# Local attention and a gated MLP in one kernel: nine zero products ahead, a padded output chunk, transposes issued two tiles ahead, and the softmax division on GpSimd with its transpose issued later

## The chip, the cores and the metric

The kernel runs on 1 core of one Trainium2 chip. The metric is the device time of one execution in microseconds (us), the median of 3 runs.

A core has five engines that run side by side and wait for one another through semaphores: PE (TensorE: matrix products; the trace shows its weight loads apart, as PEld), DVE (VectorE), ACT (ScalarE), POOL (GpSimd) and SP (SyncE, which here only issues DMAs). Each engine takes its instructions in the order in which the program lists them.

## The reference: what is computed

One input x of 2048 tokens by 512, all in bf16. Both branches read the same normalised x, and both are added to x:

```python
xn = _layernorm(x, axis=-1)
return x + _A_ref(xn, A_wqkv, A_wo) + _B_ref(xn, B_w_in, B_w_sp, B_b_sp, B_w_out)
```

- A is attention with 32 heads of 16 dimensions. A token sees itself and the 255 tokens before it. Output: `softmax(q k^T / 4) v @ wo`.
- B is a gated MLP: `z = gelu(xn @ w_in)`, 1376 columns, split into z1 and z2 of 688; z2 is normalised per token; `g = w_sp @ z2 + b_sp` mixes all 2048 tokens; output: `(z1 * g) @ w_out`.

## The kernel before

Tokens are cut into 16 tiles of 128. Pools hold the on-chip tiles; PSUM, which PE writes, is divided into three pools: `ps_s` (3 buffers, tag S: scores), `ps_y` (one buffer, tag y: projections m, attention sums o_t, outputs fo) and `ps_g` (one buffer, tag g: mixing sums gf). With one buffer, the next user of y or g has to wait until an engine has copied the last one out.

**Stage 1** (to about 61 us of the span). For each token tile n: DVE takes mean and variance of x (`x_stats`, L387 and L388), POOL raises the variance to the power -0.5 (`rs_x`, L260), DVE normalises (`norm_apply`, L392). The result is transposed to xnT, for n below 8 by four PE products with the identity and a copy by ACT (`transpose_x`, L406 and L409), from 8 on by a DMA (L401). Then 16 products per tile and 1376 columns (`do_z`, L417) with gelu on ACT (L425); DVE takes the statistics of z2 (`z2_side`, L265) and normalises it (L269). The order is written out by hand (L443 to L516): x's statistics and norm run four and three tiles ahead, PE transposes one tile ahead, and from n = 6 on one early projection of k, q or v goes between the tiles. POOL also clears a few tiles there (`small_setup`, L377 to L381).

**Stage 2** (to about 283 us) works off a list of small groups, in an order that the class `Plan` (L41) computes before the program is built, from durations written into it (`OUT_MM`, the `td` added after an attention group, `o_at` from which an output group may be placed):

- `quad(kb, G, e)`: 4 score products of 32 rows each for a key block against up to 3 query blocks, into two S tiles; ACT takes exp into E (L631).
- `mask(kb, G)`: POOL clears the upper triangle of the diagonal block (L640), DVE multiplies the far block by a mask (L645).
- `unit_av(qb, half)`: 48 small products of E and v, the softmax sums among them, into o_t (L658). DVE then runs a series of four: transposes o_t to C (L667, tile o_c), takes the reciprocal of the sums (L671, rsum), multiplies (L673, o_norm) and transposes back (L680, oT).
- `unit_k`, `unit_q`, `unit_v`: projections of 4 products of 512 columns, copied out by DVE (L290, L310, L324).
- `unit_g(n, half, c)`: one of 16 products of the mixing with w_sp (L545); after the 16th, DVE forms u = (g + b) * z1 (L552), and after the second half a DMA transposes u to uT (L559).
- `unit_out(n, part)`: part 0 is 4 products of oT with wo (L585), part 1 is 6 products of uT with w_out (L593), of which the sixth has 48 rows; DVE adds x (L597), a DMA stores.

There are 512 g, 128 quad, 64 mask, 32 av, 37 projection and 26 output groups in the list. g groups are what the plan puts in where another group would have to wait.

**Tail**: output tiles 13, 14 and 15, one after another, in S tiles.

The series that the change takes apart:

```python
        nc.vector.reciprocal(out=rsum[:], in_=c_s)
        o_n = onp.tile([P, 8, 2, DH], BF, name="o_norm")
        nc.vector.tensor_tensor(out=o_n[:], in0=..., in1=..., op=ALU.mult)
        oT = otp.tile([P, 2, P], BF, name="oT")
        nc.vector.transpose(out=..., in_=...)
```

The functions that the diff touches, with their line numbers:

Of the kernel before, what the change touches and what calls it, by code (L numbers as in the profile page):

```python
# [8 lines left out]
P = 128  # L9
BF = mybir.dt.bfloat16  # L10
F32 = mybir.dt.float32
# [8 lines left out]
FH = 688  # L20
# [11 lines left out]
EBUFS = 12  # L32
X_DMA = 8
TAIL_OUT = 3


def nblk(kb):
# [3 lines left out]
class Plan:  # L41
# [1 line left out]

    PROJ = 0.91
    AV_PAIR = 0.0165
    OUT_MM = 0.24
    GCH = 0.144
    LAT = 0.36
    BACK = 0.08
# [13 lines left out]
    def run(self, proj, n_out_inline):  # L63
# [17 lines left out]
        while qi < len(quads) or ai < len(avs) or oi < len(outs) or gi < len(gs) or proj:  # L81
# [74 lines left out]
            if pick[2] == "quad":  # L156
                kb, G, e = quads[qi]
                w = nblk(kb)
                order.append(("quad", kb, G, e))
                a, b = (2 * qi) % 3, (2 * qi + 1) % 3  # L160
                dur = {3: 0.755, 2: 0.55, 1: 0.34}[w]
                lat = self.LAT - 0.05 * (3 - w)
                for s in (a, b):
                    self.ta = max(self.ta, self.tp + lat) + dur
                    self.sfree[s] = self.ta + self.BACK
                self.tp += 0.14 + 0.054 * w
                if e == 1:
                    pend.append((self.ta + 0.05, (kb, G)))
                qi += 1
            elif pick[2] == "av":  # L170
                qb, h = avs[ai]
                order.append(("av", qb, h))
                self.tp += pick[3]
                self.yfree = self.evac(0.75)
                self.td += 0.85
                if h == 1:
                    o_at[qb] = self.td + 0.1
                av_emitted.add((qb, h))
                ai += 1
            elif pick[2] == "proj":  # L180
                p = pick[4]
                proj.remove(p)
                order.append(("proj", p[2], p[3]))
                self.tp += pick[3]
                self.yfree = self.evac({"k": 1.2, "q": 0.7, "v": 0.7}[p[2]])
                done_proj[(p[2],) + p[3]] = self.yfree
            elif pick[2] == "out":
                n, part = outs[oi]
                order.append(("out", n, part))
                self.tp += pick[3]  # L190
                if part == 1:
                    self.yfree = self.evac(0.7)
                oi += 1
            else:
                n, hf, c = gs[gi]
                order.append(("g", n, hf, c))
                self.tp += self.GCH
                if c == NB - 1:
                    self.gfree = self.evac(0.52)
                    if hf == 1:  # L200
                        u_at[n] = self.gfree + 3.0
                gi += 1
# [6 lines left out]
def kernel(  # L209
# [102 lines left out]
    def unit_v(n, on_act=False):  # L312
# [10 lines left out]
        else:  # L323
            nc.vector.tensor_copy(out=dst, in_=src)  # L324

    nc.vector.memset(fmask[:], 1.0)
    nc.vector.memset(esel[:], 1.0)
    make_identity(nc, ident[:])
    with tc.tile_pool(name="win_pool", bufs=1) as winp, tc.tile_pool(
# [19 lines left out]
        def load_win(half, c0=0, c1=NDC):  # L349
# [23 lines left out]
            out=esel[:], in_=esel[:], pattern=[[32, 4]], compare_op=ALU.is_ge,  # L373
            fill=0.0, base=DH - 1, channel_multiplier=-1,
        )
        def small_setup():
            nc.gpsimd.memset(v_ring[:, :, :, 1, :], 1.0)  # L377
            for u_sb in u_sbs:
                nc.gpsimd.memset(u_sb[:, FH:UPAD], 0.0)
            with nc.allow_non_contiguous_dma(reason="tiny bias gather"):  # L380
                nc.gpsimd.dma_start(out=b_bf[:], in_=B_b_sp.rearrange("(n p) -> p n", p=P))  # L381

        xn_tiles = {}

# [13 lines left out]
        def transpose_x(n):  # L398
            xn = xn_tiles.pop(n)
            if n >= X_DMA:  # L400
                nc.sync.dma_start_transpose(out=xnT[:, :, n * P : (n + 1) * P], in_=xn[:])  # L401
                return
            pool, tag = (ps_y, "y") if n in (1, 3) else (ps_g, "g")
            tp = pool.tile([P, NDC, P], BF, name="tp", tag=tag)
            for c in range(NDC):
                nc.tensor.transpose(  # L406
                    out=tp[:, c, :], in_=xn[:, c * P : (c + 1) * P], identity=ident[:]
                )
            nc.scalar.copy(out=xnT[:, :, n * P : (n + 1) * P], in_=tp[:])  # L409

        def do_z(n, half):
            zp2 = ps_s.tile([P, 2, 512], F32, name="zs", tag="S")
            zp = zp2[:].rearrange("p a q -> p (a q)")
            f0 = half * FH
            for c in range(NDC):
                for lo, hi in Z_RANGES:
                    nc.tensor.matmul(  # L417
                        zp[:, lo:hi],
                        lhsT=xnT[:, c, n * P : (n + 1) * P],
                        rhs=w_in_sb[:, c, f0 + lo : f0 + hi],  # L420
                        start=(c == 0),
                        stop=(c == NDC - 1),
                    )
            dst = z1_all if half == 0 else z2_all
            nc.scalar.activation(out=dst[:, n, :], in_=zp[:, 0:FH], func=ACT.Gelu_apprx_tanh)  # L425
# [40 lines left out]
        nc.sync.dma_start(  # L466
            out=w_out_sb[:, 0:5, :], in_=B_w_out[0:640, :].rearrange("(c p) n -> p c n", p=P)
        )
        nc.sync.dma_start(out=w_out_sb[0:48, 5, :], in_=B_w_out[640:688, :])
        norm_apply(2)  # L470
        rs_x(3, 4)
        do_z(0, 1)
        norm_apply(3)
        do_z(1, 1)
        small_setup()
        transpose_x(2)
        x_stats(4)
        transpose_x(3)
        rs_x(4, 5)
        nc.vector.tensor_reduce(  # L480
            out=emask[:, 0:1], in_=esel[:], op=ALU.add, axis=mybir.AxisListType.X
# [9 lines left out]
        for n in range(2, NB + 3):  # L491
            if n < NB:
                do_z(n, 1)
            if n + 3 < NB:
                norm_apply(n + 3)
                if n + 3 >= X_DMA:
                    transpose_x(n + 3)
            if 3 <= n < X_DMA - 1:
                transpose_x(n + 1)
            if n == 4:  # L500
                nc.vector.tensor_copy(out=b_all[:], in_=b_bf[:])
            if 1 <= n - 1 < NB:
                z2_side(n - 1)
            if n + 4 < NB:
                x_stats(n + 4)
                rs_x(n + 4, n + 5)
            if n >= 6 and early:
                f, a = early.pop(0)
                f(*a, on_act=True)
            if n >= 3:  # L510
                do_z(n - 3, 0)
# [60 lines left out]
    def unit_out(n, part, tail=False):  # L572
        if part == 0:
            if not tail:
                load_xres(n)
            if tail:
                t = ps_s.tile([P, 2, 512], F32, name="mt", tag="S")
                fo_tiles[n] = t[:, 0, :]
            else:
                t = ps_y.tile([P, 512], F32, name="fo", tag="y")  # L580
                fo_tiles[n] = t[:]
            fo = fo_tiles[n]
            for c in range(NDC):
                oT = oT_tiles[(n, c // 2)]
                nc.tensor.matmul(  # L585
                    fo, lhsT=oT[:, c % 2, :], rhs=wo_sb[:, c, :], start=(c == 0), stop=False
                )
            return
        fo = fo_tiles.pop(n)
        uT = uT_tiles.pop(n)  # L590
        for c in range(NFC):
            kk = P if c < NFC - 1 else FH - (NFC - 1) * P
            nc.tensor.matmul(  # L593
                fo, lhsT=uT[0:kk, c, :], rhs=w_out_sb[0:kk, c, :], start=False, stop=(c == NFC - 1)
            )
        x_ch = x_tiles.pop(n)
        nc.vector.tensor_tensor(out=x_ch, in0=fo, in1=x_ch, op=ALU.add)  # L597
        (nc.scalar if tail else nc.sync).dma_start(out=out2[n * P : (n + 1) * P, :], in_=x_ch)
        if n + 1 < NB - TAIL_OUT:
            load_xres(n + 1)  # L600

    E_tiles = {}

    def quad(kb, G, e):
        nb = nblk(kb)
# [30 lines left out]
            )  # L636

    def mask(kb, G):
        E = E_tiles[(kb, G)]
        nc.gpsimd.affine_select(  # L640
            out=E[:, 0, :, :], in_=E[:, 0, :, :], pattern=[[0, 8], [1, P]], compare_op=ALU.is_ge,
            fill=0.0, base=0, channel_multiplier=-1,
        )
        if nblk(kb) == 3:
            nc.vector.tensor_tensor(  # L645
                out=E[:, 2, :, :], in0=E[:, 2, :, :],
                in1=fmask[:].unsqueeze(1).to_broadcast([P, 8, P]), op=ALU.mult,
            )

    def unit_av(qb, half):  # L650
        T = ps_y.tile([P, 2, 2 * P], F32, name="o_t", tag="y")
        kbs = [kb for kb in (qb - 2, qb - 1, qb) if kb >= 0]
        for g2 in range(2):
# [16 lines left out]
        rsum = sml.tile([P, 2, 8], F32, name="rsum")  # L670
        nc.vector.reciprocal(out=rsum[:], in_=c_s)  # L671
        o_n = onp.tile([P, 8, 2, DH], BF, name="o_norm")
        nc.vector.tensor_tensor(  # L673
            out=o_n[:],
            in0=c_o.rearrange("p e q d -> p q e d"),
            in1=rsum[:].rearrange("p e q -> p q e").unsqueeze(3).to_broadcast([P, 8, 2, DH]),
            op=ALU.mult,
        )
        oT = otp.tile([P, 2, P], BF, name="oT")
        nc.vector.transpose(  # L680
            out=oT[:].rearrange("p g q -> p (g q)"), in_=o_n[:].rearrange("p q e d -> p (q e d)")
        )
        oT_tiles[(qb, half)] = oT

    load_wsp(0)
    load_wsp(1)
# [65 lines left out]
```

## Time and profile before

| | |
|---|---|
| median of 3 runs | 295.42 us (295.39 to 295.44) |
| the profiled execution's own time | 295.57 us |
| its span, first to last instruction | 293.9 us |
| PE busy, share of the span | 269.4 us, 92% |
| ACT busy | 218.2 us, 74% |
| DVE busy | 213.9 us, 73% |
| POOL busy | 92.8 us, 32% |
| DVE row o_norm (L673), 32 of them | 21.4 us, 668 ns mean |
| POOL row mask (L640), 64 of them | 74.7 us, 1167 ns mean |
| DVE row mask (L645), 56 of them | 47.6 us, 853 ns mean |

Lnnn is a line of the kernel before. A row such as `L673 DVE TENSOR_TENSOR o_norm<-o_c,rsum` is one kind of instruction: its line, engine, operation, what it writes and what it reads. "Idle before" is the time for which the engine did nothing just ahead of it; "<-" names what ended that. [...]

### The profile page before, as it was taken

To read this page: it belongs to the slowest core of one execution; us is meant where nothing else is said; L and a number is where in the kernel's file an instruction comes from. 1 tells how busy PE (TensorE), PEld (TensorE's weight loads), DVE (VectorE), ACT (ScalarE), POOL (GpSimd) and SP (SyncE) were. 2 spreads that over 40 slices of the span, in tenths; PEclk is the share of its full clock that TensorE was granted. 3 is DMA by queue.
4 is the path that set the end of the run, shared out by engine and by line. 5 is a ranking of instruction groups with operands and counts; after the bars stand their busy time and mean duration, and the time that the engine had idled before them with its cause. 6 is when DMAs were issued, how large, how long until landed. Compare 5 with 4: busy or idle time off the path is not lost.

```text
span 293.9 us, 7526 instructions
## 1 busy us (share of the span) xinstructions
PE 269.4 (92%) x3136; PEld 135.5 (46%) x3168; DVE 213.9 (73%) x412; ACT 218.2 (74%) x314; POOL 92.8 (32%) x102
## 2 busy tenths in 40 slices
PE   1899999999989989999998999999898999999895
PEld 0555544444435444444544453545444554545451
DVE  5877777936877685865788887866869885956681
ACT  2478756588889889988699958783797678798810
POOL 3622222203342234324143323333233312335520
PEclk9999999999999999999999999999999999999999
DMA  7991111800415242332231423144314133545103
GB/s 230 324 284 44 36 38 36 170 12 0 100 19 118 65 72 51 89 85 51 65 74 39 99 44 94 39 97 56 83 36 100 31 70 83 94 38 134 29 4 80
DMA packets 60178, 23.58 MB, mean 80 GB/s; under 512 B 51264, under 2 KB 59632, under 8 KB 60144
## 3 DMA queue, kind: packets, MB, share of 16 engines
q1 hardware_dynamic: 59664, 22.70, 34.0%
q8 instruction: 25, 0.41, 0.6%
q10 hardware_dynamic: 432, 0.39, 0.4%
q0 software_dynamic: 48, 0.00, 0.1%
q14 instruction: 9, 0.07, 0.1%
HBM read 8.41 MB, written 2.10 MB: 36 GB/s over the span
## 4 chain that ended last, share of the span: by engine, by line
PE 64%; DVE 25%; issue 4%; POOL 3%; DMA 2%; ACT 1%; SPq 0%; DVEq 0%
PE gf L545 23%; PE S L623 9%; PE o_t L658 7%; PE fo L593 7%; PE fo L585 4%; PE m L315 4%; DVE st L265 3%; PE m L300 3%; DVE o_norm L673 3%; DVE st L387 3%; DVE o_c L667 3%; PE m L277 3%; DVE E L645 3%; POOL rstdx L260 2%; PE zs L417 2%
## 5 line engine op out<-in xcount | busy, mean ns | idle before, releaser
L631 ACT ACTIVATE E<-S 128x768 bf16<-128x768 f32 (+2 forms) x256 | 178.9, 773 | 38.4 <-issue 22.6
L640 POOL TENSOR_SCALAR_AFFINE_SELECT E<-E 128x1024 bf16<-128x1024 bf16 x64 | 74.7, 1167 | 147.9 <-ACT E L631 122.3
L545 PE MATMUL gf<-z_all,wspT 128*128 128x344 bf16 x512 | 94.6, 311 | 6.1 <-DVE u_sb L552 6.1
L545 PEld LDWEIGHTS <-wspT 128*128 128x128 bf16 x512 | 44.3, 97 | 38.4 <-issue 15.8
L645 DVE TENSOR_TENSOR E<-E,fmask 128x1024 bf16<-128x1024 bf16 x56 | 47.6, 853 | 0.6
L623 PE MATMUL S<-q_ring,k_ring 32*128 32x384 bf16 (+2 forms) x576 | 45.2, 303 | 1.3 <-ACT E L631 1.2
L417 PE MATMUL zs<-w_in_sb,xnT 128*128 128x512 bf16 (+1 forms) x251 | 42.5, 318 | 2.5 <-DMA xnT<-xn 1.3
L425 ACT ACTIVATE z_all<-zs 128x688 bf16<-128x688 f32 x32 | 23.8, 744 | 17.1 <-PE zs L417 17.1
L667 DVE STREAM_TRANSPOSE o_c<-o_t 128x512 f32<-128x512 f32 x32 | 22.9, 715 | 15.2 <-PE o_t L658 14.9
L417 PEld LDWEIGHTS <-xnT 128*128 128x128 bf16 x256 | 22.7, 101 | 20.9 <-DMA xnT<-xn 3.1
L623 PEld LDWEIGHTS <-k_ring 32*128 32x128 bf16 x576 | 14.6, 91 | 38.3 <-issue 36.0
L658 PE MATMUL o_t<-E,v_ring 128*32 128x128 bf16 x1440 | 26.0, 220 | 1.0 <-DVE k_ring L290 0.8
L658 PEld LDWEIGHTS <-v_ring 128*32 128x32 bf16 x1440 | 20.9, 97 | 8.2 <-issue 7.7
L597 DVE TENSOR_TENSOR x_ch<-fo,x_ch 128x512 bf16<-128x512 f32 x13 | 9.0, 692 | 21.2 <-PE fo L593 18.6
L673 DVE TENSOR_TENSOR o_norm<-o_c,rsum 128x256 bf16<-128x256 f32 x32 | 21.4, 668 | 1.1
L593 PE MATMUL fo<-w_out_sb,uT 128*128 128x512 bf16 x78 | 20.4, 382 | 0.0
L552 DVE SCALAR_TENSOR_TENSOR u_sb<-gf,b_all,z_all 128x344 bf16<-128x344 f32 x32 | 17.9, 560 | 1.7 <-PE gf L545 1.5
L290 DVE TENSOR_TENSOR k_ring<-m,emask 128x1024 bf16<-128x1024 f32 x12 | 14.7, 1221 | 5.8 <-PE m L277 5.8
L315 PE MATMUL m<-wqkv,xnT 128*128 128x512 bf16 x53 | 15.9, 381 | 1.1 <-DVE x_ch L597 0.5
L300 PE MATMUL m<-xnT,wqkv 128*128 128x512 bf16 x58 | 16.2, 380 | 0.7 <-DVE v_ring L324 0.3
L277 PE MATMUL m<-xnT,wqkv 128*128 128x512 bf16 x57 | 16.1, 380 | 0.6 <-DVE o_c L667 0.2
L260 POOL TENSOR_TENSOR rstdx<-rs_v,negh 128x1 f32<-128x1 f32 x16 | 8.8, 550 | 23.6 <-DVE rs_v L259 22.2
(51 smaller groups left out, 175.9 us busy)
## 6 DMA issues: line engine op xcount, KB each, us to landing
xs<-in_A_x_dram SPq DMA_DIRECT2D x7, 256.0 KB, 11.3
x_ch<-in_A_x_dram SPq DMA_DIRECT2D x13, 128.0 KB, 2.2
out_dram<-x_ch SPq DMA_DIRECT2D x13, 128.0 KB, 1.7
wqkv<-in_A_wqkv_dram SPq DMA_DIRECT2D x1, 1536.0 KB, 10.9
w_in_sb<-in_B_w_in_dram SPq DMA_DIRECT2D x4, 344.0 KB, 3.9
w_out_sb<-in_B_w_out_dram SPq DMA_DIRECT2D x1, 640.0 KB, 9.8
wo_sb<-in_A_wo_dram SPq DMA_DIRECT2D x1, 512.0 KB, 11.2
xnT<-in_A_x_dram SPq DMA_DIRECT2D x3, 128.0 KB, 3.3
```

Source lines behind the costliest of these rows:

```text
L300: nc.tensor.matmul(m[:], lhsT=wqkv[:, c, G * P : (G + 1) * P], rhs=xnT[:, c, grp * 512 : (grp + 1) * 512], start=(c == 0), stop=(c == NDC ...
L315: nc.tensor.matmul(m[:], lhsT=xnT[:, c, n * P : (n + 1) * P], rhs=wqkv[:, c, 2 * D : 3 * D], start=(c == 0), stop=(c == NDC - 1),)
L417: nc.tensor.matmul(zp[:, lo:hi], lhsT=xnT[:, c, n * P : (n + 1) * P], rhs=w_in_sb[:, c, f0 + lo : f0 + hi], start=(c == 0), stop=(c == NDC ...
L545: nc.tensor.matmul(gf[:, 0:FQ], lhsT=w[:, c, :], rhs=z2_all[:, c, lo : lo + FQ], start=(c == 0), stop=(c == NB - 1),)
L593: nc.tensor.matmul(fo, lhsT=uT[0:kk, c, :], rhs=w_out_sb[0:kk, c, :], start=False, stop=(c == NFC - 1))
L623: nc.tensor.matmul(S[:, i, d0 : d0 + w], lhsT=k_ring[32 * s : 32 * s + 32, G, e, k0 : k0 + P], rhs=q_ring[32 * s : 32 * s + 32, G, s0 : s0 ...
L631: nc.scalar.activation(out=E[:, 0:nb, j : j + 3 : 2, :].rearrange("p b h c -> p h b c"), in_=tiles[pr][:, :, 0:ncol].rearrange("p h (b c) ...
L640: nc.gpsimd.affine_select(out=E[:, 0, :, :], in_=E[:, 0, :, :], pattern=[[0, 8], [1, P]], compare_op=ALU.is_ge, fill=0.0, base=0, channel_ ...
L645: nc.vector.tensor_tensor(out=E[:, 2, :, :], in0=E[:, 2, :, :], in1=fmask[:].unsqueeze(1).to_broadcast([P, 8, P]), op=ALU.mult,)
L658: nc.tensor.matmul(T[32 * s : 32 * s + 32, e, g2 * P : (g2 + 1) * P], lhsT=v_ring[:, kb % VRING, 4 * G + s, e : e + 2, :].rearrange("p a d ...
L667: nc.vector.transpose(out=C[:, 0 : 32 * DH], in_=T[:].rearrange("p e q -> p (e q)"))
L673: nc.vector.tensor_tensor(out=o_n[:], in0=c_o.rearrange("p e q d -> p q e d"), in1=rsum[:].rearrange("p e q -> p q e").unsqueeze(3).to_bro ...
```

## The change

Four edits, the first three of which are independent of the fourth.

1. Nine products of 128x512 zeros are put at the head of PE's list, into an S tile that nothing reads. Their source is a slice of xnT that DVE clears first.
2. Chunk 5 of w_out, 48 rows, is cleared by POOL to 128 rows, so that the sixth product of an output's part 1 has 128 rows. uT's rows behind the 48 come from columns of u that were zero already. `OUT_MM` in the plan goes from 0.24 to 0.222.
3. `transpose_x` by PE runs two tiles ahead, and tiles 2 and 3 are transposed between the first two `do_z`. Tile 3 uses the g buffer.
4. The product with the reciprocals goes from DVE to POOL. The transpose behind it (oT) is not issued at once: `unit_av` puts it on a list `o_late`, and `finish_o` issues it at the next `unit_av`, at the output group that needs it, or at every second mask, whichever is first. In the plan, DVE's time after an av falls from 0.85 to 0.72 and `o_at` moves 2 us later, which makes another order of the whole list.

```diff
+    nc.vector.memset(xnT[:, 3, 0:512], 0.0)
...
+        nc.gpsimd.memset(w_out_sb[:, NFC - 1, :], 0.0)
...
+        wt = ps_s.tile([P, 2, 512], F32, name="warm_t", tag="S")
+        for i in range(N_WARM):
+            nc.tensor.matmul(
+                wt[:, 0, :], lhsT=xnT[:, 3, 0:P], rhs=xnT[:, 3, 0:512], start=True, stop=True
+            )
...
-            pool, tag = (ps_y, "y") if n in (1, 3) else (ps_g, "g")
+            pool, tag = (ps_y, "y") if n == 1 else (ps_g, "g")
...
         do_z(0, 1)
+        transpose_x(2)
         norm_apply(3)
         do_z(1, 1)
+        transpose_x(3)
         small_setup()
-        transpose_x(2)
         x_stats(4)
-        transpose_x(3)
...
-            if 3 <= n < X_DMA - 1:
-                transpose_x(n + 1)
+            if n + 2 < X_DMA:
+                transpose_x(n + 2)
...
-            kk = P if c < NFC - 1 else FH - (NFC - 1) * P
             nc.tensor.matmul(
-                fo, lhsT=uT[0:kk, c, :], rhs=w_out_sb[0:kk, c, :], start=False, stop=(c == NFC - 1)
+                fo, lhsT=uT[:, c, :], rhs=w_out_sb[:, c, :], start=False, stop=(c == NFC - 1)
             )
...
-    OUT_MM = 0.24
+    OUT_MM = 0.222
...
-                self.td += 0.85
+                self.td += 0.72
                 if h == 1:
-                    o_at[qb] = self.td + 0.1
+                    o_at[qb] = self.td + 2.0
...
             fo = fo_tiles[n]
+            if any(r[0] == n for r in o_late):
+                finish_o()
...
     def mask(kb, G):
+        if o_late and kb >= 0:
+            o_age[0] += 1
+            if o_age[0] % 2 == 0:
+                finish_o()
...
     def unit_av(qb, half):
+        finish_o()
...
-        nc.vector.tensor_tensor(
+        nc.gpsimd.tensor_tensor(
             out=o_n[:],
             in0=c_o.rearrange("p e q d -> p q e d"),
             in1=rsum[:].rearrange("p e q -> p q e").unsqueeze(3).to_broadcast([P, 8, 2, DH]),
             op=ALU.mult,
         )
-        oT = otp.tile([P, 2, P], BF, name="oT")
-        nc.vector.transpose(
-            out=oT[:].rearrange("p g q -> p (g q)"), in_=o_n[:].rearrange("p q e d -> p (q e d)")
-        )
-        oT_tiles[(qb, half)] = oT
+        o_late.append((qb, half, o_n))
+
+    def finish_o():
+        while o_late:
+            qb, half, o_n = o_late.pop(0)
+            oT = otp.tile([P, 2, P], BF, name="oT")
+            nc.vector.transpose(
+                out=oT[:].rearrange("p g q -> p (g q)"), in_=o_n[:].rearrange("p q e d -> p (q e d)")
+            )
+            oT_tiles[(qb, half)] = oT
```

More of the change, by code (lines that the diff above doesn't have):

```diff
@@ L34 @@
 TAIL_OUT = 3
+N_WARM = 9
 def nblk(kb):
@@ L468 @@
         )
-        nc.sync.dma_start(out=w_out_sb[0:48, 5, :], in_=B_w_out[640:688, :])
+        nc.sync.dma_start(out=w_out_sb[0 : FH - 5 * P, 5, :], in_=B_w_out[5 * P : FH, :])
         norm_apply(2)
@@ L602 @@
     E_tiles = {}
+    o_age = [0]
     def quad(kb, G, e):
@@ L648, in mask @@
             )
+    o_late = []
     def unit_av(qb, half):
+        finish_o()
         T = ps_y.tile([P, 2, 2 * P], F32, name="o_t", tag="y")
```

## The prediction, made before the changed kernel had run

> **What bounds the kernel.** I read the page's busy times first, then the chain of waits of the whole span, then the chain in two windows, then PE's own rows. PE is busy 92% of the span, and the chain by line is led by PE rows. But the chain changes hands between two stages, so each edit has to be priced in its own stage.
>
> Stage 1, the chain in the window 42 to 62 us (start, length, what):
>
> ```profile
> 50.57 0.41 DVE xn L392
> ...
> 51.02 2.42 DMA xnT<-xn
> ...
> 53.48 1.34 PE zs L417 x8
> ...
> 57.77 3.45 PE zs L417 x23
> 61.22 0.27 PE S L623 x4
> ```
>
> The same chain asked from 8 us on shows no PE row before 53.48: from 8.98 (POOL clearing v_ring, 0.90, then the issue of a DMA, 1.27) it goes round DVE and POOL only, 3.6 us per token tile (x's statistics start at 23.37, 27.23 and 30.60), while PE's own round, seen in four early projections at 26.88, 30.07, 33.27 and 36.47, takes 3.2. PE arrives early and waits for the last transposes by DMA. After the last one it has 7.7 us of fixed work, and stage 2 starts at 61.15.
>
> Stage 2, the chain in the window 207 to 213:
>
> ```profile
> 208.18 0.73 DVE o_c L667
> ...
> 208.93 0.27 DVE rsum L671
> ...
> 209.22 1.34 DVE o_norm L673
> ...
> 210.95 0.55 DVE u_sb L552
> ...
> 211.54 1.18 PE gf L545 x7
> ```
>
> PE ended a half of the mixing at 208.6, but its u had to stand in DVE's queue behind the series of an attention group; the one g buffer was free only at 211.5, and PE stood for 1.36 us. The o_norm here took 1.34, not its usual 0.43, because POOL's mask ran at the same time (209.18 to 210.27). That this is no accident shows in o_norm's own row (ns, least/median/most):
>
> ```profile
> L673 DVE TENSOR_TENSOR o_norm<-o_c,rsum x32: 424/426/1330, 77.0 to 284.0; 128x256 bf16<-128x256 f32 x32
> ```
>
> and in the page's rows of the two masks (busy us, mean ns; the DVE one's least is 648, its most 1575; POOL's 1091 and 1628):
>
> ```profile
> L640 POOL TENSOR_SCALAR_AFFINE_SELECT E<-E 128x1024 bf16<-128x1024 bf16 x64 | 74.7, 1167 | 147.9 <-ACT E L631 122.3 <-DVE rsum L671 18.6 <-DVE u_sb L552 4.4
> L645 DVE TENSOR_TENSOR E<-E,fmask 128x1024 bf16<-128x1024 bf16 x56 | 47.6, 853 | 0.6
> ```
>
> **How much PE stands in stage 2.** From the timeline I took the usual distance from each group's first product to the next group's: g 0.1455 us, a projection or part 0 of an output 0.863, a quad 0.274 (0.286 where its queries wrap; 0.22 and 0.167 in the last two key blocks), an av 0.786 (0.34 and 0.562 at the start), part 1 of an output 1.409, and 0.096 more wherever one of the wide groups is followed by a quad or an av. With the counts of the list (512 g, 37 projections, 13 + 13 outputs, 128 quads, 32 av, 126 such changes) the sum is 205.8. Stage 2 lasted from 61.15 to 282.88, 221.7: PE stood for 15.9 us. Ten of the stands come in the 3 us behind an attention series, at 78, 104, 148, 158, 189, 210, 220, 253, 266 and 273 us: 0.64, 0.93, 0.45, 1.54, 0.63, 1.36, 1.36, 0.62, 0.30 and 0.90, together **8.7 us**. These the fourth edit can reach.
>
> **The change, edit by edit.**
>
> *Zero products.* Nine products of 512 columns. The first real ones, 16 products with 5504 columns, took 4.32 us from 7.53, the same 16 later 2.51, though the granted clock reads 1.00 throughout. At 0.785 ns a column the nine take 3.6 us; they start when DVE has cleared 512 columns, at about 1.3 (a quarter of that, fmask, takes 0.17), and end about 4.9, before the first transpose at 5.25. The clear delays esel by at most 0.5 us, and ACT, which reads it, is loading a table until 2.08. If they quicken the real ones, up to 1.8 us of PE time goes at 7.5 us; the chain there is DVE's, PE waits longer at the end of stage 1. I take 0, bounds -0.5 and +0.3.
>
> [...]
>
> *Transposes two ahead.* They take away waits of PE on ACT's copies (1.9 us of its weight loads, behind the same cover): 0. Without the cover they and the first edit would be worth at most 3.7.
>
> *Padded chunk.* PE's weight rows, before:
>
> ```profile
> 125.36 0.76 PEld L593 LDWEIGHTS <-uT 128*128 128x128 bf16 x5 [0.17 <-issue]
> 126.55 0.09 PEld L593 LDWEIGHTS <-uT 48*128 48x128 bf16 x1 [0.42 <-issue]
> 126.86 0.10 PEld L623 LDWEIGHTS <-k_ring 32*128 32x128 bf16 x4 [0.23 <-issue]
> ```
>
> From first load to the next group 1.50. Six products of equal rows at 0.216 make 1.295, plus the 0.096: 1.39. Saved 0.113 x 13 = **-1.5** in stage 2, and 0.6 in the tail, below. POOL's extra clear (512 columns; v_ring's 1024 took 0.95) falls into its idle 1.33 us before 4.14.
>
> *New order.* The list keeps its counts; changes from wide to narrow groups fall from 126 to 124, **-0.2**.
>
> *Product on POOL.* DVE loses 32 x 0.668 = 21.4 us. Behind an av, u was ready after 0.17 (wait) + 0.72 + 0.25 + 0.67 + 0.45 + 0.56 and 0.2 between them, 3.0 us; now 0.67 and 0.45 are out: 1.84. I laid 1.84 against the distance, in the new order, from each av to the next demand for the g or y buffer: it falls short at nine avs, by 1.09 and 0.83 at the last two, 0.77 at (12,1), 0.57 at (8,1), 0.39 at (0,1), 0.57 at the other four, together 4.2. So 8.7 becomes 4.2, **-4.5**.
>
> What POOL's product takes, P, no row shows. Least: a mask of 128 elements, 0.29. Most: a mask of 1024 under contention, 1.63. Between 0.29 (128 elements) and 1.09 (1024), two inputs of 256 lie at 0.63; I take 0.65. POOL's list is in order: the next mask stands behind the product, and the product waits for rsum, 1.18 after the av. A mask so queued is done 1.18 + P + 1.09 + 0.1 after the av. With P = 0.65 that is late for avs (14,1) and (15,0) by 0.5 together and for (15,1), whose mask stands straight ahead of it, by about 1.0 beyond what is counted: **+1.5**. New on DVE: at 15 of 32 avs the next DVE work is a mask's product, beside POOL's; 15 x 0.65 = 9.8 us of stretching at worst, of which I take 7% as stands (the 15.9 less 3.5 that buffers fall short even with DVE empty, to 165 us of DVE in stage 2): **+0.7**. The late oT waits for POOL, but is mostly issued one or two masks (3 to 6 us) later.
>
> [...]
>
> *Tail.* From the last g's end at 283.03 to the last add at 290.43 it is 7.40. Equal rows take 0.39 out between the tiles and 0.21 at the last, and PE's wait for the last uT (0.2 at 288.6) goes, as its u no longer stands behind o_norm. But the last oT is now issued behind the adds of tiles 13 and 14: PE has 0.43 of work and is held until 0.11 + 0.69 + 0.45 + 0.1 are over, +0.9. Together **+0.1**.
>
> Sum: -1.5 - 0.2 - 4.5 + 1.5 + 0.7 + 0.1 = -3.9. From the profiled execution's 295.57: **291.7**. It lies 0.15 above the median of 295.42, which I let stand.
>
> **Rivals.**
> - *The stands only move.* DVE gets free, but PE then waits as long for masks or the y buffer. For it: in the new order the y buffer falls short at 12 places (4.1 us) even with DVE empty, before at 9 (3.2). Only PE's own 1.7 remains: 293.9.
> - *Full relief.* All 8.7 go but the 1.9 at the last two avs, no wait for POOL: 295.57 - 1.7 - 8.7 + 1.9 + 0.1 = 287.2.
> - *POOL becomes late (slower).* With P at its upper end of 1.63, avs (6,0), (13,0), (14,0), (14,1), (15,0), (15,1) and (0,1) wait for masks by 0.83, 0.63, 0.97, 1.15, 1.3, 1.98 and 0.13, together 7.0: 295.57 - 6.2 + 7.0 + 0.8 = 297.2. It decides from P = 1.4 on, where the waits eat 5.4. For it: the same engines' rows stretch to 1.63 beside each other. Against: POOL is idle 147.9 us before masks.
> - *The zero products do not quicken anything:* the same 291.7, since the cover hides it either way.
>
> **Chances.** Forecast 0.42 (288.5 to 293.3), stands move 0.20, full relief 0.13, slower 0.20, nothing to see 0.05. The range takes both ends of P and the full relief: 287.2 to 297.2. A measurement here tells about 0.2% from no change, 0.6 us. Faster by more: 0.42 + 0.13 + 0.15 of the second case = 0.70; slower 0.18 of its 0.20; within 0.12, the rest.
>
> **What would show it.** Stage 2 starts at 61.1 again and the chain in stage 1 is DVE's; the first 16 products take about 2.5, not 4.3; L593's six are followed after 1.39; POOL has 32 rows of 0.65; PE's stands for u_sb shrink from 6.1 us. I am wrong if stage 2 starts earlier by over 0.5, if P is over 1.4, or if PE's waits for masks or for oT grow beyond 3.

## The result, and the profile after

The changed kernel takes **297.43 us** (median of 6 runs, 296.64 to 298.88) against 295.43 (6 runs of the kernel before beside it, 295.39 to 296.51): ratio 1.0071, 95% interval 1.0052 to 1.0091. It is slower by 0.7%. The forecast was 291.7, with 297.2 as the range's end and 0.70 for faster.

The profiled execution took 297.72 with a span of 296.0, 2.15 more than the one before. The first view is the page of the changed kernel, busy time by engine and the groups that the prediction priced (busy us, mean ns of one | idle just before, and what ended it):

```profile
PE 274.6 (93%) x3177; PEld 136.4 (46%) x3177; DVE 190.5 (64%) x381; ACT 218.2 (74%) x314; POOL 115.2 (39%) x135
...
L656 POOL TENSOR_SCALAR_AFFINE_SELECT E<-E 128x1024 bf16<-128x1024 bf16 x64 | 74.9, 1175 | 51.2 <-ACT E L643 51.1
...
L692 POOL TENSOR_TENSOR o_norm<-o_c,rsum 128x256 bf16<-128x256 f32 x32 | 22.6, 707 | 74.3 <-DVE rsum L690 74.3
L661 DVE TENSOR_TENSOR E<-E,fmask 128x1024 bf16<-128x1024 bf16 x56 | 47.0, 840 | 2.6 <-ACT E L643 2.6
...
L704 DVE STREAM_TRANSPOSE oT<-o_norm 128x256 bf16<-128x256 bf16 x32 | 14.0, 438 | 7.3 <-POOL o_norm L692 7.3
```

DVE is relieved as was meant, 213.9 to 190.5 us, and the means of the two masks' rows have moved by less than 2% (1167 to 1175 ns on POOL, 853 to 840 on DVE). Yet the time rose: how busy DVE is in total did not decide it. Stage 1 ends as before (chain of waits, window 42 to 62: start, length, what):

```profile
51.23 2.42 DMA xnT<-xn
53.64 0.05 issue
53.69 1.34 PE zs L427 x8
...
57.92 3.50 PE zs L427 x24
61.42 0.27 PE S L635 x4
```

It is 0.2 later than before and led by the same DMA. The loss is in stage 2, which took 223.46 against 221.73. I took it apart as the prediction did, into the sum of PE's usual group distances and the stands (the time that PE stands still beyond them):

| stage 2, us | before | after |
|---|---|---|
| sum of usual distances | 205.70 | 204.03 |
| stands at a half's first g (the g buffer) | 7.47 | 5.29 |
| stands at an av, a projection or an output (the y buffer) | 6.67 | 8.74 |
| inside an av, waiting for a mask | 0 | 1.17 |
| outputs waiting for oT | 0 | 0.90 |
| S tiles | 0.53 | 0.18 |
| the rest (small ones; after, some 1.3 of a lowered clock) | 1.36 | 3.16 |

So PE's own work fell by 1.67 and its stands rose by 3.41. What stood in DVE's queue is to be seen at the longest of them. Timeline of the changed kernel (start, length, engine, line; in brackets the idle time before and what ended it):

```profile
249.84 0.25 DVE L690 RECIPROCAL rsum<-o_c 128x16 f32<-128x16 f32 x1
...
250.24 0.64 POOL L692 TENSOR_TENSOR o_norm<-o_c,rsum 128x256 bf16<-128x256 f32 x1 [3.60 <-DVE rsum L690]
...
250.83 2.59 POOL L656 TENSOR_SCALAR_AFFINE_SELECT E<-E 128x1024 bf16<-128x1024 bf16 x2
250.92 0.45 DVE L704 STREAM_TRANSPOSE oT<-o_norm 128x256 bf16<-128x256 bf16 x1 [0.82 <-POOL o_norm L692]
...
251.29 1.18 DVE L661 TENSOR_TENSOR E<-E,fmask 128x1024 bf16<-128x1024 bf16 x1
252.39 0.56 DVE L562 SCALAR_TENSOR_TENSOR u_sb<-gf,b_all,z_all 128x344 bf16<-128x344 f32 x1
...
253.01 0.73 PE L555 MATMUL gf<-z_all,wspT 128*128 128x344 bf16 x2 [1.85 <-DVE u_sb L562]
```

Here oT was issued straight behind rsum, because this mask happened to be an even one. DVE idled 0.82 us for POOL, then worked off oT and the mask's product, stretched to 1.18 beside POOL's mask, while u, for which PE stood 1.85 us, was third in the queue. The same place then shows something else (each line a window: its length, the busy time of PE, PEld, DVE, ACT and POOL with the number of instructions, the granted clock, the DMA share, GB/s):

```profile
250.00:252.00 2.00, 1.16 (x8) 0.39 (x7) 1.18 (x3) 2.00 (x4) 1.76 (x3) 1.00 0.00 0
252.00:254.00 2.00, 0.99 (x6) 0.21 (x5) 2.00 (x4) 0.75 (x2) 1.42 (x1) 0.66 0.00 0
254.00:256.00 2.00, 2.00 (x14) 0.79 (x14) 0.15 (x1) 1.51 (x2) 0.00 (x0) 0.50 0.63 128
256.00:258.00 2.00, 2.00 (x59) 1.25 (x58) 1.09 (x3) 0.82 (x2) 0.00 (x0) 0.99 1.07 233
```

Windows cut at 249.2, 252.6 and 256.0 show it more sharply: PE is busy 1.66 of 3.40 us at a clock of 1.00, then 2.99 of 3.40 at 0.50, then the clock is back at 0.99. The clock fell within the stand (0.57 from 252.6 to 252.8, 0.50 from 252.8 on), and the groups from 253.0 to 256.7 lasted 1.3 us longer than usual: as I read it, the stand cost a second time. This explains only a part: the three executions at a mean clock of 1.00 took 296.64, 296.84 and 297.14, still 1.2 to 1.7 above the kernel before.

### The profile page after: what moved, and what is told of

It reads as the page before. It is cut to its first block, busy times and chain, and to the rows that moved or that the text cites. A ratio compares the mean times of both kernels' runs of the same rounds, so it can differ in the third digit from the quotient of the medians.

```text
span 296.0 us, 7545 instructions
## 1 busy us (share of the span) xinstructions
PE 274.6 (93%) x3177; PEld 136.4 (46%) x3177; DVE 190.5 (64%) x381; ACT 218.2 (74%) x314; POOL 115.2 (39%) x135
## 4 chain that ended last, share of the span: by engine, by line
PE 70%; DVE 18%; POOL 4%; issue 3%; DMA 2%; ACT 1%; SPq 0%; POOLq 0%; DVEq 0%
PE gf L555 25%; PE S L635 10%; PE o_t L677 7%; PE fo L604 6%; PE m L316 4%; PE fo L597 4%; PE zs L427 4%; PE m L278 4%; PE m L301 3%; DVE st L266 3%; DVE st L397 2%; POOL rstdx L261 2%; DVE o_c L686 2%; DVE xn L402 2%; DVE E L661 1%
## 5 line engine op out<-in xcount | busy, mean ns | idle before, releaser
L555 PE MATMUL gf<-z_all,wspT 128*128 128x344 bf16 x512 | 95.6, 313 | 4.3 <-DVE u_sb L562 4.1
L656 POOL TENSOR_SCALAR_AFFINE_SELECT E<-E 128x1024 bf16<-128x1024 bf16 x64 | 74.9, 1175 | 51.2 <-ACT E L643 51.1
L692 POOL TENSOR_TENSOR o_norm<-o_c,rsum 128x256 bf16<-128x256 f32 x32 | 22.6, 707 | 74.3 <-DVE rsum L690 74.3
L661 DVE TENSOR_TENSOR E<-E,fmask 128x1024 bf16<-128x1024 bf16 x56 | 47.0, 840 | 2.6 <-ACT E L643 2.6
L604 PE MATMUL fo<-w_out_sb,uT 128*128 128x512 bf16 x78 | 19.1, 381 | 0.0
L704 DVE STREAM_TRANSPOSE oT<-o_norm 128x256 bf16<-128x256 bf16 x32 | 14.0, 438 | 7.3 <-POOL o_norm L692 7.3
L301 PE MATMUL m<-xnT,wqkv 128*128 128x512 bf16 x64 | 16.5, 380 | 1.2 <-DVE v_ring L325 0.9
L278 PE MATMUL m<-xnT,wqkv 128*128 128x512 bf16 x64 | 16.5, 380 | 0.6 <-DVE v_ring L325 0.6
## 6 DMA issues: line engine op xcount, KB each, us to landing
xs<-in_A_x_dram SPq DMA_DIRECT2D x7, 256.0 KB, 10.2
```

Of the source, the lines that this page charges most:

```text
L278: nc.tensor.matmul(m[:], lhsT=wqkv[:, c, D + G * P : D + (G + 1) * P], rhs=xnT[:, c, grp * 512 : (grp + 1) * 512], start=(c == 0), stop=(c ...
L301: nc.tensor.matmul(m[:], lhsT=wqkv[:, c, G * P : (G + 1) * P], rhs=xnT[:, c, grp * 512 : (grp + 1) * 512], start=(c == 0), stop=(c == NDC ...
L555: nc.tensor.matmul(gf[:, 0:FQ], lhsT=w[:, c, :], rhs=z2_all[:, c, lo : lo + FQ], start=(c == 0), stop=(c == NB - 1),)
L604: nc.tensor.matmul(fo, lhsT=uT[:, c, :], rhs=w_out_sb[:, c, :], start=False, stop=(c == NFC - 1))
L656: nc.gpsimd.affine_select(out=E[:, 0, :, :], in_=E[:, 0, :, :], pattern=[[0, 8], [1, P]], compare_op=ALU.is_ge, fill=0.0, base=0, channel_ ...
L661: nc.vector.tensor_tensor(out=E[:, 2, :, :], in0=E[:, 2, :, :], in1=fmask[:].unsqueeze(1).to_broadcast([P, 8, P]), op=ALU.mult,)
```

## The experiments

The theories: **W**, the place of oT (DVE waits for POOL, and what is queued behind oT is late); **O**, the new order of the list; **P**, POOL's product itself; **C**, the zero products, the early transposes or the clock. In each table row the time before is that of runs on the same chip in the same batch; ratios are to it.

### 1. Which edit loses the time

`e1_edits123`: the product back on DVE, oT at once, old plan.

```diff
-        nc.gpsimd.tensor_tensor(
+        nc.vector.tensor_tensor(
...
         o_late.append((qb, half, o_n))
+        finish_o()
...
-    OUT_MM = 0.222
+    OUT_MM = 0.24
...
-                self.td += 0.72
+                self.td += 0.85
...
-                    o_at[qb] = self.td + 2.0
+                    o_at[qb] = self.td + 0.1
```

> Edits 1 to 3 alone: zero products, padded chunk, transposes two ahead; the product with the reciprocals is on DVE again with the transpose straight behind it, and the list has the order of before. Theory W (the fourth edit makes DVE wait for POOL: oT idles 7.3 us on DVE in the changed kernel, and that takes back what the shorter series gives): the rows of the padding hold, 13 x 0.113 in stage 2 and 0.6 in the tail, less the 0.2 by which stage 1 is longer: 293.6. Theory O (the new order of the list loses, through the y buffer): the same 293.6. Theory C (the zero products and the early transposes themselves cost, and the slow clock at 252 to 256 us comes with them): 295.5 or more.

`e2_order_only`: the kernel before, with the plan's three new constants and nothing else (the last six lines above, signs exchanged).

> The kernel before with nothing but the three changed constants of the plan, so with the changed kernel's order of the list; the whole series is on DVE. Theory O: this alone is slower, 297 to 298.5, since the stands ahead of y's next user go from 6.5 us in the profile before to 8.6 in the one after. Theory W: the order alone is worth little, 295 to 296.

`e3_old_order`: the changed kernel with the old three constants (the same six lines as they stand).

> All four edits, with the plan's constants and so the order of before. Theory O: without the new order the relief shows: 291 to 292.5. Theory W: DVE still waits for POOL, and six transposes are asked for by an output group one mask behind: 294 to 296.

`e4_two_masks`: the changed kernel, but the count of masks begins anew at each av, so that oT is never issued at the first mask behind it.

```diff
     def unit_av(qb, half):
         finish_o()
+        o_age[0] = 0
```

> The changed kernel, but the masks are counted anew at each attention group, so that oT is never issued at the first mask behind its own group (6 of 32 were); 3 still stand straight ahead of the next group. Theory W: some of the 7.3 us of waiting goes and with it the stand of 1.9 at 251 us: 295 to 296, and fewer of the executions with a lower clock. Theory O: 297 as before, within 0.3.

| | us (least to most) | ratio to before (295.22 to 299.35, median 296.03) |
|---|---|---|
| edits 1 to 3 | 293.89 (293.75 to 294.47) | 0.9922 [0.9904, 0.9940] |
| order alone | 298.90 (297.24 to 300.47) | 1.0085 [1.0059, 1.0111] |
| all edits, old order | 294.77 (294.23 to 296.52) | 0.9962 [0.9933, 0.9990] |
| all edits, two masks later | 294.91 (293.71 to 295.03) | 0.9942 [0.9921, 0.9964] |

Edits 1 to 3 gain 2.1 us, what the prediction gave them. The order loses by itself, 2.9 us, on a kernel whose product is still on DVE: O holds. One line that only moves oT makes the changed kernel faster than the one before: W holds as well. In the old order the stands at the g buffer fell to 2.26, but outputs now waited 3.39 us, and the trace shows for what (timeline of `e3_old_order`):

```profile
85.45 0.68 DVE L661 TENSOR_TENSOR E<-E,fmask 128x1024 bf16<-128x1024 bf16 x1
...
86.05 0.57 DVE L562 SCALAR_TENSOR_TENSOR u_sb<-gf,b_all,z_all 128x344 bf16<-128x344 f32 x1
...
86.53 0.43 DVE L704 STREAM_TRANSPOSE oT<-o_norm 128x256 bf16<-128x256 bf16 x1
...
87.02 0.11 PEld L597 LDWEIGHTS <-oT 128*128 128x128 bf16 x2 [1.34 <-DVE oT L704]
87.03 0.60 PE L597 MATMUL fo<-wo_sb,oT 128*128 128x512 bf16 x2 [0.85 <-DVE oT L704]
```

In the old order 7 of 13 output groups stand 3.2 to 3.6 us behind their av, by the usual distances, and here oT is issued only on the output's account, behind a mask's product and a u in DVE's queue. The rule "every second mask" is early where DVE has other work and late where an output needs it.

### 2. Order and place crossed

`e5_old_timed` and `e6_new_timed`: all edits, in the old and the new order; oT is issued ahead of the first group that lies more than 1.8 us of list time behind its av, and no more at masks.

```diff
-        if o_late and kb >= 0:
-            o_age[0] += 1
-            if o_age[0] % 2 == 0:
-                finish_o()
...
+    took = {"quad": 0.27, "g": 0.146, "av": 0.79, "proj": 0.9, "out": 1.1, "mask": 0.0}
+    since = 0.0
     for i, op in enumerate(order):
+        if since > 1.8:
+            finish_o()
+        since = 0.0 if op[0] == "av" else since + took[op[0]]
```

> All four edits and the order of before, but oT is issued by the list's own time: ahead of the first group that stands over 1.8 us (0.146 for a g, 0.27 for a quad, 0.79 for an av, 0.9 for a projection) behind its attention group. In the run with the old order and oT at every second mask the g buffer's stands fell from 7.5 to 2.3 us, but 3.4 us came back in output groups that waited for their oT. Theory W (the place of oT decides): both are had, 290.5 to 292. Theory P (the product on POOL itself loses, by masks that come late or by the shared work): no better than edits 1 to 3 alone, 293.5 or more.

> The changed kernel, new order, with oT by the same rule of 1.8 us. Theory W with O (place of oT and order both cost): like the run with two masks, 294 to 295, and 2 to 3 above the same rule in the old order. Theory W alone: within 0.7 of the same rule in the old order.

`e7_pad_only`: the kernel before with the padded chunk and nothing else.

```diff
+        nc.gpsimd.memset(w_out_sb[:, NFC - 1, :], 0.0)
...
-                fo, lhsT=uT[0:kk, c, :], rhs=w_out_sb[0:kk, c, :], start=False, stop=(c == NFC - 1)
+                fo, lhsT=uT[:, c, :], rhs=w_out_sb[:, c, :], start=False, stop=(c == NFC - 1)
```

> The kernel before with the padded chunk alone (no zero products, transposes one ahead, the whole series on DVE, old order). The forecast's claim that zero products and early transposes are worth 0: 293.5 to 294, like edits 1 to 3 together. If they were worth something: 0.5 or more above those three.

`e8_new_dve`: `e1_edits123` with the three new constants.

> Edits 1 to 3 and the new order, with the product on DVE and oT straight behind it: the changed kernel without the move to POOL. Theory O: the order costs as much here as it did on the kernel before, so 2 to 3 above edits 1 to 3 alone: 296 to 297, and the move to POOL with oT at every second mask then gave nothing. Theory W: at most 1 above them, 294.5 to 295.

| us | old order | new order | the order costs |
|---|---|---|---|
| product on DVE, edits 1 to 3 | 293.89 | 298.75 (298.08 to 299.11) | 4.9 |
| on POOL, oT by masks | 294.77 | 297.43 | 2.7 |
| on POOL, oT by list time | **290.21** (289.82 to 290.68) | 293.62 (293.26 to 293.80) | 3.4 |

`e5_old_timed` has ratio 0.9780 [0.9757, 0.9804] and `e6_new_timed` 0.9894 [0.9873, 0.9914]; both beat the kernel before and the changed one. Padding alone is 294.38, 0.9929 [0.9906, 0.9953]. By the ratio that is the same as edits 1 to 3 together (0.9922; in microseconds 0.5 more, but the kernel before was 0.8 slower in that batch): the zero products and early transposes are worth nothing that can be measured, and with `e5_old_timed` theories C and P fall.

Some cells of the table come from different batches, whose times before differ by up to 1.4 us. By the ratios the order costs 4.3, 3.2 and 3.4 in the three rows (2 to 3 had been expected for the first). Down the columns, moving the product gains 3.7 in the old order (4.2 by the ratios) if oT is well placed, and loses 0.9 in the same batch (294.77 against 293.89) if it is not. From the second row to the third, the place of oT alone is worth 4.6 in the old order and 3.8 in the new one (5.4 and 5.2 by the ratios). PE's waits show both failures. First the kernel before, then the changed one, then `e5_old_timed` (who waited for whom: us in total, times, longest):

```profile
PE gf L545 <- DVE u_sb L552: 6.1, 10, 1.3
```

```profile
DVE oT L704 <- POOL o_norm L692: 7.3, 11, 0.8
...
PE gf L555 <- DVE u_sb L562: 4.1, 5, 1.9
...
PEld L597 <- DVE oT L704: 2.4, 2, 1.2
...
PE o_t L677 <- DVE x_ch L608: 1.2, 2, 0.9
PE o_t L677 <- DVE k_ring L291: 1.2, 1, 1.2
```

```profile
DVE oT L700 <- POOL o_norm L688: 9.1, 14, 0.8
...
PE gf L555 <- DVE u_sb L562: 1.0, 2, 0.8
```

The reader is to see that DVE's waits for POOL are longer in the fast kernel (9.1) than in the changed one (7.3). The length of that wait is not the cost; what stands behind it in the queue can be.

### 3. What in the order costs

Each constant by itself, on `e5_old_timed` (one of the three new lines each), and one more thing, the last oT ahead of the tail:

```diff
+    finish_o()
     for n in range(NB - TAIL_OUT, NB):
         unit_out(n, 0, tail=True)
```

> As the version with all edits, the old order of the list and oT placed by list time (290.2), but with one of the plan's three new constants: OUT_MM 0.222. Asked of this run and the next two: which constant makes the new order cost its 3.4 us (293.6 against 290.2). Worked from the orders alone, with DVE doing nothing but what sits between a group and its buffer, y falls short by 3.2 us in the old order, 4.1 in the new one, 2.8 here, and g by 0.34, 1.46 and 1.07; at the end of the list 17 mixing groups stand in a row behind the last av (1 in the old order, 31 in the new). Theory O (the order costs where a buffer falls short): -0.4 + 0.7, so 290.5. Rival (any other order than that of before costs, since the constants of before had been fitted to it): 292 or more. Third (the constant carries nothing, the late o_at carries all): 290.2.

> As the version at 290.2, but with td 0.72 in place of 0.85 after an av and nothing else. The plan then believes that DVE is free 0.13 us earlier behind each av and places the next user of y earlier. Theory O: y falls short by 3.44 against 3.21, g by 1.07 against 0.34, so about +1.0: 291.2. If the constant is right about the time that DVE is now free of the product, the order should cost nothing: 290.2. Rival (any other order costs): 292 or more.

> As the version at 290.2, but with o_at 2.0 us behind the av in place of 0.1 and nothing else: output groups are placed later in the list. Theory O: y falls short by 3.85 against 3.21, g by 0.73 against 0.34, so +1.0: 291.2; outputs that are late meet the next av at the one y buffer, so waits ahead of av and projections should grow, and waits of outputs for oT (0.5 us in the version at 290.2) should go. Rival (o_at carries the whole cost of the order): 293.6. Third (it is of use, as it was meant): 289.8.

> As the version at 290.2, but the last oT is issued ahead of the tail's output groups, so that it stands ahead of the adds of output tiles 13 and 14 in DVE's queue and not behind them. Theory: it was worked out that PE is held 0.9 us for that oT in the tail; issued earlier it waits only for POOL's product, which is done before: 289.3. Rival: the adds of tiles 13 and 14 are short and the tail is set by the last u, so nothing moves: 290.2. If the oT now holds DVE for POOL ahead of the last u: 290.5 or more.

Measured: OUT_MM 292.42 (291.76 to 292.81), td 293.18 (292.77 to 293.59), o_at 291.90 (291.36 to 292.10), tail 290.00 (289.74 to 290.14; 0.9805 [0.9790, 0.9819]). The three miss what I had worked out from the places where the y and g buffers fall short (the "shortfall") by 0.7 to 2.0, and the tail misses 289.3: from the last g of stage 2 to the end it is 0.34 shorter, and there the tail's first wait for uT takes over (0.36 us). My bookkeeping of buffers thus did not explain the order. A simple count did: how many g groups the plan leaves in a row behind the last av, which are 1, 31, 17, 17 and 15 in the old order, the new one and these three. A g left over, 0.1455 us, is one that no earlier wait was covered with. Four more orders of the same work, all on `e12_tail`, were chosen to cross that count with the shortfall (only the three constants differ, as the table says).

> Which feature of an order costs? All four of these kernels are the version at 290.0 (last oT ahead of the tail) with other constants in the plan, so that its list comes out in another order. Known: 1 mixing group left in a row behind the last av and a y shortfall of 3.2 us worked from the order, 290.0; 31 left and 4.1, 293.6. Here OUT_MM 0.228, td 0.6, o_at 2.5: 1 left, y shortfall 5.2, 500 of 757 places differ. Theory L (a mixing group left over at the end, 0.146 us, is lost as cover earlier: 30 x 0.146 = 4.4 for the new order, 2.3 and 2.0 with one constant, against 3.4 and 1.7 to 3.0 measured): 290.0 again, within 0.6. Theory Y (what the y and g buffers fall short by, worked from the order): 290.0 + 2.0 + 0.2 = 292.2. Theory F (any other order costs, as the constants were fitted to the old one): 292 or more.

> OUT_MM 0.24, td 0.78, o_at 2.0: 1 mixing group left behind the last av, y shortfall 1.9, g shortfall 0, 530 of 757 places differ. Theory L: 290.0 within 0.6. Theory Y: 290.0 - 1.3 - 0.3 = 288.4. Theory F: 292 or more.

> Only td goes from 0.85 to 0.78, and 31 mixing groups are left behind the last av; y shortfall 2.7, g shortfall 1.5, 628 of 757 places differ. Theory L: 290.0 + 30 x 0.146 = 294.4, or 293.4 with the size measured for the new order. Theory Y: 290.0 - 0.5 + 1.1 = 290.6. Theory F: 292 or more.

> OUT_MM 0.252, td 0.78, o_at 0.3: no mixing group left behind the last av, y shortfall 2.0, g shortfall 0, 506 of 757 places differ. Theory L: 289.9 within 0.6. Theory Y: 288.5. Theory F: 292 or more.

| OUT_MM, td, o_at | g left | y shortfall | expected by L / by Y | measured |
|---|---|---|---|---|
| 0.24, 0.85, 0.1 (`e12_tail`) | 1 | 3.2 | | 290.00 |
| 0.228, 0.6, 2.5 | 1 | 5.2 | 290.0 / 292.2 | 289.43 (289.22 to 289.61) |
| 0.24, 0.78, 2.0 | 1 | 1.9 | 290.0 / 288.4 | **287.46** (287.37 to 287.54) |
| 0.24, 0.78, 0.1 | 31 | 2.7 | 293.4 / 290.6 | 293.42 (293.09 to 293.77) |
| 0.252, 0.78, 0.3 | 0 | 2.0 | 289.9 / 288.5 | 308.30 (307.40 to 308.81) |

(L is the theory of the count, Y that of the shortfall.) The second and the fourth row, where the two pull apart most, decide for the count. Two orders that differ from the old one in 500 and more places are fast, so it isn't that the constants of before were fitted. But the count isn't all: the third row is the fastest kernel of all, ratio 0.9706 [0.9683, 0.9729], 2.5 below what the count gave it. Its stands at the y buffer are 3.87 us against 5.78 in `e12_tail`, 1.9 of the 2.5. Why they are shorter is not shown: the shortfall as worked out from the order does not sort the three rows with one g left (5.2 gives 289.43, 3.2 gives 290.00). With 31 left, two whole halves of the mixing follow one another with nothing between (`e15_31_y27`, timeline):

```profile
275.83 2.36 PE L555 MATMUL gf<-z_all,wspT 128*128 128x344 bf16 x15
...
278.23 0.58 DVE L562 SCALAR_TENSOR_TENSOR u_sb<-gf,b_all,z_all 128x344 bf16<-128x344 f32 x1
278.86 2.49 PE L555 MATMUL gf<-z_all,wspT 128*128 128x344 bf16 x16 [0.67 <-DVE u_sb L562]
```

DVE takes u as soon as the last g of the half has ended, and PE stands all the same, twice 0.83 us by the distances (0.67 in the bracket is the idle time of its rows); the rest of the loss must lie earlier, at waits that had no g to fill them.

The last row refutes the count as a law. There no g was left behind the last four avs either; the mixing had run ahead of its own data (`e16_none_y20`, timeline; then windows as above):

```profile
239.54 1.46 PE L604 MATMUL fo<-w_out_sb,uT 128*128 128x512 bf16 x6
...
241.03 1.21 SPq L569 DMA_TRANSPOSE uT<-u_sb  x1
...
242.29 2.03 SPq L540 DMA_TRANSPOSE wspT<-in_B_w_sp_dram  x1
246.51 1.28 PEld L555 LDWEIGHTS <-wspT 128*128 128x128 bf16 x6 [5.48 <-DMA wspT<-in_B_w_sp_dram]
...
256.00 1.47 PE L604 MATMUL fo<-w_out_sb,uT 128*128 128x512 bf16 x6
...
257.50 1.21 SPq L569 DMA_TRANSPOSE uT<-u_sb  x1
...
259.39 0.42 SPq L579 DMA_DIRECT2D x_ch<-in_A_x_dram  x1
...
262.94 0.69 DVE L608 TENSOR_TENSOR x_ch<-fo,x_ch 128x512 bf16<-128x512 f32 x1 [6.87 <-DMA x_ch<-in_A_x_dram]
...
263.68 1.47 PE L673 MATMUL o_t<-E,v_ring 128*32 128x128 bf16 x48 [4.65 <-DVE x_ch L608]
```

```profile
242.00:243.00 1.00, 0.00 (x0) 0.00 (x0) 0.32 (x1) 0.87 (x2) 0.00 (x0) 1.00 0.83 163
243.00:244.00 1.00, 0.00 (x0) 0.00 (x0) 0.00 (x0) 0.00 (x0) 0.00 (x0) 0.83 0.29 61
244.00:245.00 1.00, 0.00 (x0) 0.00 (x0) 0.00 (x0) 0.00 (x0) 0.00 (x0) 0.50 1.05 240
...
246.00:250.00 4.00, 3.49 (x13) 1.28 (x14) 0.00 (x0) 1.11 (x2) 0.00 (x0) 0.50 0.00 0
```

Both times uT's transpose left SP's queue right when an output's part 1 had ended (at 241.00 and 257.47); the program has two uT buffers, so I read this as a wait for a free one. What stood behind it in the queue came late: first the next w_sp tile, for which the mixing stood 5.3 us by the distances, then the output's x, for which the add, and with it the next av at the y buffer, stood 4.7. The clock went to 0.50 each time (from 244.0, and from 262 to 266), and the last avs had no cover at all. Cover is to be spent evenly, neither saved nor used up.

## Why the prediction was wrong

- **Stage 1, zero products, early transposes: right**, 0 as forecast. In the profiled execution the zero products did not bring full speed for the first tile: its 8 products from 7.70 took 2.50, and full speed (1.33) came at 10.36. The two times 8 together, 3.83, are 0.49 less than the 4.32 of the first 16 before, and stage 2 still began 0.2 later (61.42 against 61.22): the cover hides the gain, as was forecast.
- **Padding: right.** From first load to the next group 1.40 (129.78 to 131.18), forecast 1.39; PE's sum fell by 1.67, forecast 1.5 + 0.2.
- **POOL's product: right.** Taken at 0.65; median 0.64, at most 0.95. The rival "POOL becomes late" gave nearly the measured time, 297.2, but by luck: it needs a product of 1.4 or more.
- **Masks late, +1.5: about right**, 1.17 inside avs. **DVE stretched, +0.7: not seen** in the mean; DVE's mask went from 853 to 840 ns. **Tail, +0.1: 0.2.**
- **The step that failed first: "New order. The list keeps its counts; ... -0.2".** I valued an order by its counts of groups and changes of width. It costs 2.7 to 4.9 in four pairs of kernels. The prediction laid DVE's 1.84 us against the new order, but only for the stands behind avs; the other 7.2 us of stands it carried over from the old list, where other waits are covered by other g groups. It had noted that the y buffer falls short by 4.1 against 3.2, and used that in a rival only; the stands at the y buffer rose from 6.67 to 8.74.
- **The step that failed second: "is mostly issued one or two masks (3 to 6 us) later".** The count of masks runs on over all avs: of 32 oT, 15 went out at the second mask, 6 at the first, 2 on an output's account, 8 at the next av and 1 in the tail. 11 made DVE wait for POOL. This place of oT costs 3.8 in the new order (297.43 against 293.62) and 4.6 in the old one; the sum had nothing for it. So of the 4.5 us that the shorter series was to save, the g buffer gave 2.2 (7.47 to 5.29), while in the old order with oT placed by time it gave 5.7 (7.48 to 1.81). Moving the product was worth 3.7 there, more than the 2.3 (4.5 - 1.5 - 0.7) that I gave it.
- A lowered clock, some 1.3 us in the profiled execution, was in no step. In the changed kernel it came behind 3.4 us in which PE was busy 1.66, with no gap over 1.85 us; in `e16_none_y20` the clock was falling by 244.0 (0.83 from 243.0 to 244.0), 2.7 us after PE's last product ended (241.27). Which rule the clock follows is not shown.

Of the rivals, "the stands only move" named the mechanism (DVE free, PE waits elsewhere as long) and put it at 293.9, without the order's price; 297.4 needs both failed steps: without the new order the kernel takes 294.77, without the rule of masks 293.62, without either 290.21. None of the prediction's signs of being wrong came (stage 2 began 0.2 later, P was 0.64, PE's waits for masks and oT in stage 2 were 1.17 and 0.90): they did not watch the y buffer.

Open: how far the two failed steps would share the loss in the fastest order. The changed kernel's oT rule, and the product on DVE, each in the order of `e14_few_y19`, have no measured time; so of the 287.46 it is not shown how much is the order's alone. Nor is it shown which single earlier waits lose their cover; the count sorts eight of nine orders by time (1 left: 287.5 to 290.2; 15 to 17: 291.9 to 293.2; 31: 293.4 and 293.6) and explains no one wait.

## What to carry to other kernels

When a change touches the constants of a planner, price the new order as a change of its own: build it alone, or compare how evenly the filler work is spent, before you carry over any wait of the old one. Handing a step to another engine adds a wait where its result is taken up; place that by time since the producer (1.8 us served here; no other value was measured), and ask what is queued behind it, since the length of the wait itself says little (7.3 us in the slow kernel, 9.1 in a fast one). A busier or a freer engine is no reason for a time: DVE went from 73% to 64%, and only the waits of PE told the outcome.

## What the runs showed of the hardware

- In the changed kernel, 3.4 us with PE busy 1.66 (249.2 to 252.6) were followed by a granted clock of 0.50 for the next 3.4 us, in which PE was busy 2.99; then the clock was 0.99.
- In `e16_none_y20` PE's last product ended at 241.27; the clock read 1.00 until 243.0, 0.83 from there to 244.0 and 0.50 from 244.0 to 245.0.
- In the kernel before, 2.06 busy of 3.40 (209.2 to 212.6) and 1.85 of 3.40 (218.4 to 221.8) were followed by 3.40 us at a clock of 1.00. These few stretches show no threshold.
- POOL's product of 128x256 from f32 took 0.64 us in the median (0.43 on DVE before). In 8 of 32 it took 0.89 to 0.95; DVE's mask product ran beside each of these.
